# Grouped-query attention with a KV cache on one core: larger transfers, and outputs gathered by four units into token rows

## The chip, the core and the metric

The kernel runs on 1 core of one Trainium2 chip. A core has TensorE (PE; its weight loads are listed as PEld), VectorE (DVE), ScalarE (ACT), GpSimd (POOL) and SyncE (SP, which only issues transfers here), and 16 DMA engines that all transfers share. The metric is the device time of one execution in microseconds (us); less is better.

## The reference

One block of attention over a cache: 8 sequences, 4 new tokens each, model width 512, 32 query heads and 8 heads of K and V (so four query heads share one), 2048 cached positions, head width 128, all bf16. K and V are 32 MiB each, wq and wo 4 MiB each.

```python
B, Sq, D = 8, 4, 512; Hq, Hkv, Sk, Dh = 32, 8, 2048, 128; rep = Hq // Hkv
q = (x @ wq).reshape(B, Sq, Hq, Dh).transpose(0, 2, 1, 3)
k = jnp.repeat(k_cache, rep, axis=1)
v = jnp.repeat(v_cache, rep, axis=1)
scores = jnp.einsum("bhqd,bhkd->bhqk", q, k) * (Dh ** -0.5)
p = softmax(scores, axis=-1)
o = jnp.einsum("bhqk,bhkd->bhqd", p, v)
out = o.transpose(0, 2, 1, 3).reshape(B, Sq, Hq * Dh) @ wo
```

## The kernel before, in words

The work is cut into 8 units: two groups `gg` of four KV heads (G = 4) times four pairs `bp` of sequences (NB = 2). A unit reads 4 MiB of K and 4 MiB of V. The positions of one head are spread over 32 partitions, 64 positions (C) each, so a K or V transfer brings 16 KB to each of 128 partitions.

**Transfers.** All loads are issued by SP, in the order of the list `loads` (L118 to L123): K of unit 0 for its first sequence, x, wq in two halves, the rest of K 0, K 1, and then V of unit u and K of unit u+2 in turn; V of the last unit goes in quarters, wo comes last. Each lands in one of eight slots of 2 MiB of `ring`; `issue` (L125) lets a load go out when its slot's last reader is behind it. The issuing instruction waits on SP until that reader has finished.

**One unit.** `turn` (L162) transposes a piece of K on VectorE, eight pieces of 1.2 us a unit, into six buffers `kt`. `scores` (L185) multiplies them on TensorE with `q_bd`, which holds the queries of a unit in block-diagonal form; `queries` (L172) fills it on GpSimd. `top` (L199) takes the negated maximum on VectorE, `exps` (L221) the exponentials on ScalarE with their sums, `weights` (L235) transposes them on VectorE (`pt`) and copies them into the block-diagonal `p_bd`: of four row groups, three are copied by ScalarE and one by GpSimd. `norm` (L247) inverts the sums. `values` (L255) multiplies with V on TensorE, 64 matmuls a unit, and `scaled` (L272) applies the inverted sums on ScalarE, from PSUM into `o_sb`. `by_heads` (L280) and `to_rows` (L287) bring the result of each unit into `oP` by two matmuls with the permutation `perm`, a copy and a transpose on VectorE; `project` (L298) multiplies with wo.

**Order.** The order is written out by hand: each engine runs its instructions in the order in which the code issues them, and waits on semaphores set by their operands. In iteration u of the main loop (L341) stand the turns and scores of unit u, by_heads of unit u-2, the queries of unit u+1, top, to_rows of unit u-2, exps, weights and norm of unit u, and then values and scaled of unit u-1. So on ScalarE `scaled` of unit u-1 comes after the copies of unit u, and on VectorE the turns of unit u+1 follow norm of unit u. After the loop come the projection of the first head group, the last unit's by_heads and to_rows, the rest of the projection, and the output in two transfers.

Of the kernel before, what the change touches and what calls it, by code (L numbers as in the profile page):

```python
# [12 lines left out]
ALU = mybir.AluOpType  # L13
# [4 lines left out]
def kernel(  # L18
# [31 lines left out]
    DH = D // 2  # L50
    scale = float(Dh) ** -0.5
# [13 lines left out]
    NS = 8  # L65
    pad = ring_pool.tile([128, 192], BF16, name="pad")
    ring = ring_pool.tile([128, NS, C * Dh], BF16, name="ring")
# [3 lines left out]
    perm = const.tile([128, NB, 128], BF16, name="perm")  # L71
# [4 lines left out]
    oP = [const.tile([128, G, 4, NP, NB * Sq], BF16, name=f"oP{i}") for i in range(NG)]  # L76
# [11 lines left out]
    def load_kv(kind, u, b):  # L88
        gg, bp = units[u]
        src = (k_cache if kind == "k" else v_cache)[NB * bp + b, G * gg : G * gg + G]  # L90
        nc.sync.dma_start(  # L91
            ring[:, take((kind, u, b)), :], src.rearrange("g (s c) d -> (g s) (c d)", c=C)
        )

    def load_last_v(u):
        gg, bp = units[u]
        slots = [take(("v", u, b)) for b in range(NB)]
        for h in range(2):
            for b in range(NB):
                src = v_cache[NB * bp + b, G * gg : G * gg + G]  # L100
                nc.sync.dma_start(
                    ring[:, slots[b], h * CH * Dh : (h + 1) * CH * Dh],
                    src.rearrange("g (s c) d -> (g s) (c d)", c=C)[:, h * CH * Dh : (h + 1) * CH * Dh],
                )

    def load_wq(h):
        rows = wq.rearrange("(p r) n -> p (r n)", r=R)
        n = C * Dh
        nc.sync.dma_start(ring[:, take(("wq", h)), :], rows[:, h * n : (h + 1) * n])  # L109

    def load_wo(gg, cuts):
        slot = take(("wo", gg))
        rows = wo[gg * G * 512 : (gg + 1) * G * 512, :].rearrange("(k p r) j -> p k (r j)", k=G, r=4)
        to = ring[:, slot, :].rearrange("p (k n) -> p k n", k=G)
        for g0, g1, r0, r1 in cuts:
            nc.sync.dma_start(to[:, g0:g1, r0 * D : r1 * D], rows[:, g0:g1, r0 * D : r1 * D])

    loads = [("k", 0, 0), ("x",), ("wq", 0), ("wq", 1), ("k", 0, 1), ("k", 1, 0), ("k", 1, 1)]  # L118
    for u in range(NU):
        if u + 2 < NU:  # L120
            loads += [("v", u, 0), ("v", u, 1), ("k", u + 2, 0), ("k", u + 2, 1)]
    loads += [("v", NU - 2, 0), ("v", NU - 2, 1), ("vlast", NU - 1), ("wo", 0), ("wo", 1)]
    loads.reverse()  # L123

    def issue(done):  # L125

        while loads:
            what = loads[-1]
            if what[0] != "x" and n_loads[0] + (what[0] == "vlast") >= done + NS:
                return  # L130
            loads.pop()
            if what[0] in "kv":
                load_kv(*what)
            elif what[0] == "x":
                nc.sync.dma_start(x_sb[:, :], x.flatten_outer_dims())  # L135
            elif what[0] == "wq":
                load_wq(what[1])
            elif what[0] == "vlast":
                load_last_v(what[1])
            elif what[1] == 0:  # L140
                load_wo(0, [(0, 4, 0, 4)])
            else:
                load_wo(1, [(0, 1, 0, 4), (1, 2, 0, 4), (2, 3, 0, 4), (3, 4, 0, 2), (3, 4, 2, 4)])

    issue(0)
# [7 lines left out]
    by_row = ident[:, :].rearrange("k (g b r s) -> k b r g s", g=G, b=NB, r=rep)  # L153
    for b in range(NB):
        nc.gpsimd.tensor_copy(
            out=perm[:, b, :].rearrange("k (r g b s) -> k b r g s", r=rep, g=G, b=NB)[:, b],
            in_=by_row[:, b],
        )
# [3 lines left out]
    def turn(u, b, t):  # L162

        kt = ktpool.tile([128, CT, J, S, 2], BF16, tag="kt", name="kt")
        n = CT * Dh
        nc.vector.transpose(  # L166
            out=kt[:, :, :, :, :].rearrange("w c j s e -> w (c j s e)").bitcast(FP32),
            in_=ring[:, slot_of["k", u, b], t * n : (t + 1) * n].bitcast(FP32),
        )
        kts[u, b, t] = kt  # L170
# [28 lines left out]
    def top(u, h):  # L199
        if h == 0:  # L200
            stats[u] = [small.tile([128, n], FP32, tag=f"stat{i}", name=f"stat{i}") for i, n in enumerate((2, 1, 2, 1))]
        nc.vector.tensor_reduce(  # L202
            out=stats[u][0][:, h : h + 1],
            in_=s_ps[:, 2 * h : 2 * h + 2, :].rearrange("q t n -> q (t n)"),
            axis=AX,
            op=ALU.max,
            negate=True,
        )
        if h == 1:
            nc.vector.tensor_scalar(  # L210
                out=stats[u][1][:, :],
                in0=stats[u][0][:, 0:1],
                scalar1=stats[u][0][:, 1:2],
                scalar2=scale,
                op0=ALU.min,
                op1=ALU.mult,
            )
# [17 lines left out]
    def weights(u, h):  # L235
        pt = small.tile([128, CH // 2, 32, 2], BF16, tag="pt", name="pt")
        nc.vector.transpose(  # L237
            out=pt[:, :, :, :].rearrange("s c q e -> s (c q e)").bitcast(FP32),
            in_=ps[u, h][:, :, :, :].rearrange("q c s e -> q (c s e)").bitcast(FP32),
        )  # L240
        pb = pbs[u, h] = p_bd[(2 * u + h) % 4]
        for g in range(G):
            rows = slice(g * 32, (g + 1) * 32)
            copy = nc.gpsimd.tensor_copy if g == G - 1 else nc.scalar.copy
            copy(out=pb[rows, :, g, :, :], in_=pt[rows, :, :, :])  # L245

    def norm(u):  # L247
        nc.vector.tensor_tensor(
            out=stats[u][3][:, :], in0=stats[u][2][:, 0:1], in1=stats[u][2][:, 1:2], op=ALU.add
        )  # L250
        nc.vector.reciprocal(stats[u][3][:, :], stats[u][3][:, :])
# [3 lines left out]
    def values(u, h):  # L255
        if h == 0:
            o_pss[u] = psum_o.tile([128, NB, Dh], FP32, tag="o", name="o_ps")
        a, b = (slot_of["v", u, i] for i in range(NB))
        v = (ring[:, a : b + 1 : b - a, :] if b > a else ring[:, a : (b - 1 if b else None) : b - a, :])
        v = v.rearrange("p b (c d) -> p b c d", d=Dh)  # L260
        for i in range(CH):
            nc.tensor.matmul(  # L262
                o_pss[u][:, :, :],
                lhsT=pbs[u, h][:, i // 2, :, :, i % 2].rearrange("s g q -> s (g q)"),
                rhs=v[:, :, h * CH + i, :],
                start=(h == 0 and i == 0),
                stop=(h == 1 and i == CH - 1),
            )
# [3 lines left out]
    def scaled(u):  # L272
        o_sb = o_sbs[u] = small.tile([128, NB, Dh], BF16, tag="o_sb", name="o_sb")
        nc.scalar.activation(  # L274
            out=o_sb[:, :, :], in_=o_pss[u][:, :, :], func=COPY, scale=stats[u][3][:, :]
# [4 lines left out]
    def by_heads(u):  # L280
        o_pm = o_pms[u] = psum_m.tile([128, Dh], FP32, tag="m", name="o_pm")
        for b in range(NB):
            nc.tensor.matmul(  # L283
                o_pm[:, :], lhsT=perm[:, b, :], rhs=o_sbs[u][:, b, :], start=(b == 0), stop=(b == NB - 1)
            )

    def to_rows(u):  # L287
        gg, bp = units[u]
        o_r = small.tile([128, 4, 32], BF16, tag="o_r", name="o_r")
        nc.vector.tensor_copy(  # L290
            out=o_r[:, :, :], in_=o_pms[u][:, :].rearrange("q (d r) -> q r d", r=4)
        )
        nc.vector.transpose(
            out=oP[gg][:, :, :, bp, :].rearrange("d g r t -> d r g t"),
            in_=o_r[:, :, :].rearrange("q r d -> q (r d)"),
        )

    def project(gg, g, r0, n):  # L298
        w = ring[:, slot_of["wo", gg], :].rearrange("p (k r j) -> p k r j", k=G, r=4)
        for r in range(r0, r0 + n):  # L300
            for half in range(2):
                nc.tensor.matmul(  # L302
                    out_ps[half * T : (half + 1) * T, :],
                    lhsT=oP[gg][:, g, r, :, :].rearrange("d p t -> d (p t)"),
                    rhs=w[:, g, r, half * DH : (half + 1) * DH],
                    start=(gg == 0 and g == 0 and r == 0),
                    stop=(gg == NG - 1 and g == G - 1 and r == 3),
# [10 lines left out]
    for gg in range(NG):  # L318
        psq = psum_o.tile([128, rep * Dh], FP32, tag="o", name="psq")
        for r in range(R):  # L320
            w = ring[:, slot_of["wq", r // 2], :].rearrange("p (r n) -> p r n", r=2)[:, r % 2, :]
# [19 lines left out]
    for u in range(NU + 1):  # L341
        if u < NU:
# [5 lines left out]
            if u >= 2:  # L348
                by_heads(u - 2)
# [4 lines left out]
            if u >= 2:  # L354
                to_rows(u - 2)
# [5 lines left out]
        if u >= 1:  # L361
            values(u - 1, 0)
            if u == NU:
                by_heads(u - 2)
                to_rows(u - 2)
            values(u - 1, 1)
            scaled(u - 1)
        issue(4 + 4 * u)
    project(0, 0, 0, 4)
    project(0, 1, 0, 4)  # L370
    by_heads(NU - 1)
    to_rows(NU - 1)
    project(0, 2, 0, 4)
    project(0, 3, 0, 4)
    for g in range(G):
        project(1, g, 0, 4)
# [35 lines left out]
```

## Time and profile before

| | |
|---|---|
| time, median of 3 runs | 191.75 us (186.32 to 191.85) |
| time of the profiled execution | 186.44 us |
| span of the profiled execution | 184.3 us |
| mean granted TensorE clock | 0.953 |
| busy: TensorE, VectorE, ScalarE, GpSimd | 136.6, 117.3, 78.2, 36.2 us |
| moved by DMA | 75.71 MB, 411 GB/s over the span |
| transfers issued by SP | 16 of K, 18 of V, 2 of wq, 6 of wo, 1 of x, 1 of the output |

The span runs from the first to the last instruction; the execution's time also holds what lies around it. A slice line of the page cuts the span into 40 equal slices of 4.6 us and gives the busy share in tenths. A line of the timeline gives start, duration, engine, source line, operation, output and inputs, and in brackets how long the engine stood idle before it and which instruction ended that.

### The profile page before, as it was taken

To read this page: it belongs to the slowest core of one execution; us is meant where nothing else is said; L and a number is where in the kernel's file an instruction comes from. 1 tells how busy PE (TensorE), PEld (TensorE's weight loads), DVE (VectorE), ACT (ScalarE), POOL (GpSimd) and SP (SyncE) were. 2 spreads that over 40 slices of the span, in tenths; PEclk is the share of its full clock that TensorE was granted. 3 is DMA by queue.
4 is the path that set the end of the run, shared out by engine and by line. 5 is a ranking of instruction groups with operands and counts; after the bars stand their busy time and mean duration, and the time that the engine had idled before them with its cause. 6 is when DMAs were issued, how large, how long until landed. Compare 5 with 4: busy or idle time off the path is not lost.

```text
span 184.3 us, 2298 instructions
## 1 busy us (share of the span) xinstructions
PE 136.6 (74%) x884; PEld 81.5 (44%) x884; DVE 117.3 (64%) x147; ACT 78.2 (42%) x93; POOL 36.2 (20%) x92
## 2 busy tenths in 40 slices
PE   0001799039997998989759994989498949997992
PEld 0000233013683376338523771368135823486880
DVE  6680290689649976977488666976497549661110
ACT  2000200494079219905950298019900891059410
POOL 8500420080025005200800061005200210003000
PEclk9999999957999999999987999999979996999999
DMA  5999999999999999999999999999999999999980
GB/s 192 430 430 434 437 423 437 427 430 430 427 437 430 425 434 420 439 430 430 427 427 434 427 443 427 423 430 427 444 427 430 430 420 441 414 430 409 421 344 11
DMA packets 6586, 75.71 MB, mean 411 GB/s; under 512 B 720, under 2 KB 816, under 8 KB 1968
## 3 DMA queue, kind: packets, MB, share of 16 engines
q1 hardware_dynamic: 6528, 75.55, 96.6%
q8 instruction: 7, 0.11, 0.2%
q10 hardware_dynamic: 48, 0.02, 0.0%
q14 instruction: 3, 0.02, 0.0%
HBM read 75.53 MB, written 0.03 MB: 410 GB/s over the span
## 4 chain that ended last, share of the span: by engine, by line
DMA 68%; DVE 12%; PE 9%; issue 4%; ACT 3%; POOL 1%; SPq 1%; ACTq 0%; DVEq 0%; POOLq 0%
DMA ring<-in_k_cache_dram 43%; DMA ring<-in_v_cache_dram 17%; PE s_ps L189 9%; DVE kt L166 8%; DMA ring<-in_wo_dram 8%; DVE stat L202 3%; ACT p_sb L223 2%; POOL p_bd L245 1%; DVE pt L237 1%; SPq L109 1%; DVE stat L210 0%; SPq L135 0%; PE out_ps L302 0%; SPq L91 0%; ACT out_sb L379 0%
## 5 line engine op out<-in xcount | busy, mean ns | idle before, releaser
L189 PE MATMUL s_ps<-kt,q_bd 128*128 128x512 bf16 x256 | 70.5, 420 | 23.9 <-DVE kt L166 10.3
L166 DVE STREAM_TRANSPOSE kt<-ring 128x1024 f32<-128x1024 f32 x64 | 73.5, 1210 | 11.9 <-DMA ring<-in_k_cache_dram 11.9
L262 PE MATMUL o_ps<-ring,p_bd 128*128 128x256 bf16 x512 | 57.3, 272 | 3.2 <-DMA ring<-in_v_cache_dram 2.0
L189 PEld LDWEIGHTS <-q_bd 128*128 128x128 bf16 x256 | 25.9, 103 | 67.5 <-issue 31.6
L262 PEld LDWEIGHTS <-p_bd 128*128 128x128 bf16 x512 | 49.8, 98 | 9.9 <-issue 4.1
L223 ACT ACTIVATE p_sb<-s_ps,stat 128x1024 bf16<-128x1024 f32 x16 | 22.0, 1402 | 75.5 <-DVE stat L210 75.5
L245 ACT COPY p_bd<-pt 32x1024 bf16<-32x1024 bf16 x48 | 49.9, 1040 | 0.5
L245 POOL COPY p_bd<-pt 32x1024 bf16<-32x1024 bf16 x16 | 16.6, 1038 | 115.7 <-DVE pt L237 113.2
L202 DVE TENSOR_REDUCE stat<-s_ps 128x1 f32<-128x1024 f32 x16 | 18.9, 1220 | 13.3 <-PE s_ps L189 13.3
L237 DVE STREAM_TRANSPOSE pt<-p_sb 128x512 f32<-128x512 f32 x16 | 11.4, 711 | 15.0 <-ACT p_sb L223 15.0
L178 POOL COPY q_bd<-qT 32x64 bf16<-32x64 bf16 x64 | 13.0, 229 | 15.4 <-DVE qT L334 13.6
L323 PE MATMUL psq<-ring,xT_sb 128*32 128x512 bf16 x32 | 3.8, 626 | 8.2 <-DMA ring<-in_wq_dram 8.2
L290 DVE CAST o_r<-o_pm 128x128 bf16<-128x128 f32 x8 | 2.3, 284 | 10.1 <-PE o_pm L283 10.1
L314 PE MATMUL xtp<-ident,x_sb 32*128 32x32 bf16 x4 | 0.3, 192 | 8.9 <-DMA x_sb<-in_x_dram 8.9
L149 DVE MEMSET p_bd<- 128x2048 uint32 x3 | 5.3, 1765 | 2.0 <-PEq L396 1.2
L334 DVE STREAM_TRANSPOSE qT<-q_sb 128x64 f32<-128x64 f32 x8 | 1.2, 212 | 7.9 <-ACT q_sb L330 7.9
L330 ACT CAST q_sb<-psq 128x512 bf16<-128x512 f32 x2 | 1.2, 585 | 11.2 <-PE psq L323 11.2
L323 PEld LDWEIGHTS <-xT_sb 128*32 128x32 bf16 x32 | 1.2, 129 | 10.0 <-issue 9.5
L274 ACT ACTIVATE o_sb<-o_ps,stat 128x256 bf16<-128x256 f32 x8 | 3.8, 474 | 4.1 <-issue 3.9
L302 PE MATMUL out_ps<-ring,oP 128*32 128x256 bf16 x64 | 4.1, 273 | 0.2 <-DMA ring<-in_wo_dram 0.2
L314 PEld LDWEIGHTS <-x_sb 32*128 32x128 bf16 x4 | 0.2, 114 | 8.9 <-DMA x_sb<-in_x_dram 8.9
L302 PEld LDWEIGHTS <-oP 128*32 128x32 bf16 x64 | 3.0, 96 | 1.1 <-issue 0.6
(20 smaller groups left out, 21.9 us busy)
## 6 DMA issues: line engine op xcount, KB each, us to landing
ring<-in_k_cache_dram SPq DMA_DIRECT2D x16, 2048.0 KB, 27.1
ring<-in_v_cache_dram SPq DMA_DIRECT2D x14, 2048.0 KB, 30.1
ring<-in_wq_dram SPq DMA_DIRECT2D x2, 2048.0 KB, 14.1
ring<-in_v_cache_dram SPq DMA_DIRECT2D x4, 1024.0 KB, 29.4
ring<-in_wo_dram SPq DMA_DIRECT2D x1, 2048.0 KB, 26.9
ring<-in_wo_dram SPq DMA_DIRECT2D x3, 512.0 KB, 22.1
ring<-in_wo_dram SPq DMA_DIRECT2D x2, 256.0 KB, 15.7
x_sb<-in_x_dram SPq DMA_DIRECT2D x1, 32.0 KB, 7.7
```

What stands on the lines that cost most here:

```text
L149: nc.vector.memset(t[:, :, :, :, :], 0.0)
L166: nc.vector.transpose(out=kt[:, :, :, :, :].rearrange("w c j s e -> w (c j s e)").bitcast(FP32), in_=ring[:, slot_of["k", u, b], t * n : ( ...
L178: nc.gpsimd.tensor_copy(out=qb[rows, b, :, g, b, :].rearrange("w (j e) q -> w j e q", e=2), in_=qT[rows, gg, :, NB * bp + b, :, :, :].rear ...
L189: nc.tensor.matmul(s_ps[:, t, :], lhsT=q_bd[u % 2][:, b, 2 * j + e, :, :, :].rearrange("w g b q -> w (g b q)"), rhs=kts[u, b, t][:, :, j, ...
L202: nc.vector.tensor_reduce(out=stats[u][0][:, h : h + 1], in_=s_ps[:, 2 * h : 2 * h + 2, :].rearrange("q t n -> q (t n)"), axis=AX, op=ALU.max,
L223: nc.scalar.activation(out=p_sb[:, :, :, :].rearrange("q c s e -> q c e s"), in_=s_ps[:, 2 * h : 2 * h + 2, :].rearrange("q t (c e s) -> q ...
L237: nc.vector.transpose(out=pt[:, :, :, :].rearrange("s c q e -> s (c q e)").bitcast(FP32), in_=ps[u, h][:, :, :, :].rearrange("q c s e -> q ...
L245: copy(out=pb[rows, :, g, :, :], in_=pt[rows, :, :, :])
L262: nc.tensor.matmul(o_pss[u][:, :, :], lhsT=pbs[u, h][:, i // 2, :, :, i % 2].rearrange("s g q -> s (g q)"), rhs=v[:, :, h * CH + i, :], st ...
L274: nc.scalar.activation(out=o_sb[:, :, :], in_=o_pss[u][:, :, :], func=COPY, scale=stats[u][3][:, :])
L302: nc.tensor.matmul(out_ps[half * T : (half + 1) * T, :], lhsT=oP[gg][:, g, r, :, :].rearrange("d p t -> d (p t)"), rhs=w[:, g, r, half * D ...
L323: nc.tensor.matmul(psq[g * T : (g + 1) * T, :], lhsT=xT_sb[:, r, :], rhs=w[:, (gg * G + g) * rep * Dh : (gg * G + g + 1) * rep * Dh], star ...
```

## The change

- A load of K or V brings both sequences of the unit, 4 MiB in one transfer, into one of four slots of 4 MiB; wq comes in one transfer of 32 KB a partition.
- The first K is issued as two halves of its first sequence, then x in four transfers of 12, 10, 6 and 4 rows, then wq, then its second sequence. The last V is issued in two halves of the positions, both sequences in each.
- wo lies with 16 rows a partition (16 KB); its first half comes in one transfer, its second in four.
- `norm` multiplies the inverted sums with `of_b`, a mask of which rows belong to which sequence. `scaled` scales the first sequence's half on ScalarE, and VectorE then scales the second half and adds the first: one instruction that reads ScalarE's output.
- `by_heads` becomes `by_tokens`: four matmuls, one for each query head of a group, that accumulate four units in one PSUM tile. `to_rows` runs once for four units, over 512 columns, and `oP` holds 16 row groups for all 32 tokens.
- In the last unit one of the copies into `p_bd` goes from ScalarE to VectorE.

The order of the calls in the main loop stays as it was, but for to_rows.

```diff
-    NS = 8
+    NS = 4
-    ring = ring_pool.tile([128, NS, C * Dh], BF16, name="ring")
+    ring = ring_pool.tile([128, NS, NB, C * Dh], BF16, name="ring")
...
+    def load_kv(kind, u, parts):
         gg, bp = units[u]
+        slot = take((kind, u))
+        src = (k_cache if kind == "k" else v_cache)[NB * bp : NB * bp + NB, G * gg : G * gg + G]
+        rows = src.rearrange("b g (s c) d -> (g s) b (c d)", c=C)
+        n = C * Dh
+        for b0, b1, h0, h1 in parts:
+            h0, h1 = int(h0 * n), int(h1 * n)
+            yield nc.sync.dma_start(ring[:, slot, b0:b1, h0:h1], rows[:, b0:b1, h0:h1])
+
+    def load_x():
+        rows = x.flatten_outer_dims()
+        t = 0
+        for n in (12, 10, 6, 4):
+            nc.sync.dma_start(x_sb[t : t + n, :], rows[t : t + n, :])
+            t += n
+
+    def load_wo():
+        slot = take("wo")
+        for gg, cuts in ((0, (0, RW)), (1, (0, 8, 12, 14, 16))):
+            rows = wo[gg * G * 512 : (gg + 1) * G * 512, :].rearrange("(p r) j -> p (r j)", r=RW)
+            for r0, r1 in zip(cuts, cuts[1:]):
+                nc.sync.dma_start(ring[:, slot, gg, r0 * D : r1 * D], rows[:, r0 * D : r1 * D])
+
+    loads = ["k0", "wq", ("k", 1)]
     for u in range(NU):
+        loads.append(("v", u))
+        if u + 2 < NU:
+            loads.append(("k", u + 2))
+    loads.append("wo")
...
     for b in range(NB):
+        nc.vector.tensor_reduce(
+            out=of_b[:, b : b + 1],
+            in_=ident[:, :].rearrange("k (g b q) -> k b g q", g=G, b=NB)[:, b],
+            axis=mybir.AxisListType.XY,
+            op=ALU.add,
         )
...
             copy = nc.gpsimd.tensor_copy if g == G - 1 else nc.scalar.copy
+            if u == NU - 1 and g == 1:
+                copy = nc.vector.tensor_copy
             copy(out=pb[rows, :, g, :, :], in_=pt[rows, :, :, :])
...
+        nc.vector.reciprocal(stats[u][4][:, :], stats[u][4][:, :])
+        nc.vector.tensor_scalar_mul(stats[u][3][:, :], of_b[:, :], stats[u][4][:, :])
...
     def scaled(u):
         o_sb = o_sbs[u] = small.tile([128, NB, Dh], BF16, tag="o_sb", name="o_sb")
         nc.scalar.activation(
-            out=o_sb[:, :, :], in_=o_pss[u][:, :, :], func=COPY, scale=stats[u][3][:, :]
+            out=o_sb[:, 0, :], in_=o_pss[u][:, 0, :], func=COPY, scale=stats[u][3][:, 0:1]
+        )
+        nc.vector.scalar_tensor_tensor(
+            out=o_sb[:, 1, :],
+            in0=o_pss[u][:, 1, :],
+            scalar=stats[u][3][:, 1:2],
+            in1=o_sb[:, 0, :],
+            op0=ALU.mult,
+            op1=ALU.add,
         )
...
-    def by_heads(u):
+    def by_tokens(u):
+        gg, bp = units[u]
+        if bp == 0:
+            o_pms[gg] = psum_m.tile([128, rep, Dh], FP32, tag="m", name="o_pm")
+        w = 32 - NB * Sq - bp * NB * Sq
+        for r in range(rep):
             nc.tensor.matmul(
+                o_pms[gg][:, r, :],
+                lhsT=perm[:, r, w : w + 128],
+                rhs=o_sbs[u][:, 1, :],
+                start=(bp == 0 and r == 0),
+                stop=(bp == NP - 1),
+                skip_group_check=True,
             )
 
+    def to_rows(gg):
+        o_r = q_sb[:, 0, :, :, :, :].rearrange("k r j w e -> k (r j w e)")
         nc.vector.tensor_copy(
+            out=o_r.rearrange("k (r h g) -> k h g r", r=RW, h=rep),
+            in_=o_pms[gg][:, :, :].rearrange("k h (g r) -> k h g r", r=RW),
+        )
+        nc.vector.transpose(out=oP[gg][:, :, :].rearrange("k r t -> k (r t)"), in_=o_r)
...
             if u >= 2:
-                by_heads(u - 2)
+                by_tokens(u - 2)
...
-            if u >= 2:
-                to_rows(u - 2)
+            if u >= 2 and units[u - 2][1] == NP - 1:
+                to_rows(units[u - 2][0])
...
             values(u - 1, 1)
             scaled(u - 1)
-        issue(4 + 4 * u)
+        issue(2 + 2 * u)
```

Lines of the changed kernel that the prediction names: the turns are L182, the ScalarE and VectorE halves of scaled L291 and L294, the copies into p_bd L263.

## The prediction

> **What bounds the kernel now.** I read the slices of the page first, then the timeline of single units, because an average over the span hides who waits for whom.
>
> ```profile
> DVE  6680290689649976977488666976497549661110
> DMA  5999999999999999999999999999999999999980
> GB/s 192 430 430 434 437 423 437 427 430 430 427 437 430 425 434 420 439 430 430 427 427 434 427 443 427 423 430 427 444 427 430 430 420 441 414 430 409 421 344 11
> ```
>
> The DMA engines are full from the second slice to the last but one, at about 430 GB/s; no engine is. So the transfers set the end now: 75.55 MB at 430 GB/s is 175.7 us of the span of 184.3. A unit (8 MiB of K and V) takes 19.4 us of it: in the timeline the turns (L166) that wait for K start at 92.67, 112.07 and 131.53 us.
>
> Next question: how long would a unit take if data were never late? The timeline of units 3 and 4:
>
> ```profile
> 72.30 9.11 DVE L166 STREAM_TRANSPOSE kt<-ring 128x1024 f32<-128x1024 f32 x8
> ...
> 77.55 0.47 ACT L274 ACTIVATE o_sb<-o_ps,stat 128x256 bf16<-128x256 f32 x1
> ...
> 82.53 2.36 DVE L202 TENSOR_REDUCE stat<-s_ps 128x1 f32<-128x1024 f32 x2 [1.12 <-PE s_ps L189]
> 83.01 7.15 PE L262 MATMUL o_ps<-ring,p_bd 128*128 128x256 bf16 x64 [0.41 <-DMA ring<-in_v_cache_dram]
> ...
> 85.25 1.40 ACT L223 ACTIVATE p_sb<-s_ps,stat 128x1024 bf16<-128x1024 f32 x1 [7.23 <-DVE stat L210]
> ...
> 87.94 6.30 ACT L245 COPY p_bd<-pt 32x1024 bf16<-32x1024 bf16 x6
> ...
> 89.01 1.23 DVE L166 STREAM_TRANSPOSE kt<-ring 128x1024 f32<-128x1024 f32 x1
> ...
> 92.67 8.01 DVE L166 STREAM_TRANSPOSE kt<-ring 128x1024 f32<-128x1024 f32 x7 [2.43 <-DMA ring<-in_k_cache_dram]
> ...
> 94.27 0.47 ACT L274 ACTIVATE o_sb<-o_ps,stat 128x256 bf16<-128x256 f32 x1
> ```
>
> (Columns: start, duration, engine, line, operation, count, idle time before it and what ended it.) The reader should see three things. VectorE is free for the next unit's turns at 89.01, as soon as its softmax work is done. ScalarE is not: its six copies into p_bd run to 94.24, and only behind them comes `scaled` (L274) at 94.27, though its matmuls (L262) ended at 90.16. And nobody is held by that late L274: its reader, by_heads on TensorE, stands behind the next scores. This overlap (turns on VectorE while ScalarE copies) is why compute alone needs only 16.7 us a unit (turns start at 55.57 and 72.30, with the data there already) and can wait for DMA.
>
> **The change, part by part.**
>
> *Larger transfers, wq in one, wo in long rows.* The bytes are the same. The trace's packet records give 611 ns for 16 KB, 309 for 8 KB, 159 for 4 KB and 84 for 2 KB, on each of 16 engines. wo goes from 896 of 4 KB and 256 of 2 KB (10.25 us of the 16 engines) to 128 of 16 KB, 128 of 8 KB, 128 of 4 KB and 256 of 2 KB (9.98): 0.27 us saved. There are 14 transfers fewer, each with a 9 ns completion packet per engine: 0.13. K in halves costs 0.06. So -0.3 us, if transfers set the end. Waiting for 4 MiB in place of 2 delays one turn of eight, since the second turn already needed the other sequence.
>
> *Head.* x takes four issues for one, 0.41 us each on SP (all the SP queue behind moves 1.2 us, plus 0.4 for the second half of K), hidden while the first K's 2 MiB still lands (to 8.67 us; without that cover 1.6 us). Eight copies into perm and a wider memset on POOL: under 2 us (copies of 237 ns now), in the 13.6 us that POOL idles before L178. Two small reductions (of_b) on VectorE stand before the first turn; that turn's product is not needed until 23.3. But wq in one transfer moves eight matmuls (1.04 us at 13.63) behind its landing at 18.47: q, POOL's query copies and the first scores come about 0.9 us later. With the new multiplication in norm (about 0.2, as L210) unit 1's first turn goes from 38.44 to 39.5 (bounds 38.6 and 40.1).
>
> *scaled in two, half of it on VectorE.* This decides. ScalarE scales sequence 0 (128x128), then VectorE multiplies sequence 1 and adds ScalarE's result. In the built program both stand at the end of the iteration: on ScalarE behind the six copies, as before; on VectorE behind norm(u) and **ahead of the eight turns of unit u+1**, and the instruction waits for ScalarE. Queued behind it on VectorE are these turns; scores on TensorE wait for the turns, the maximum for the scores, exp for the maximum, the copies for exp, and the next scaled for the copies. The overlap closes into a loop, priced from rows, from first turn S to first turn of the next unit:
>
> - S to the start of the maximum (L202): 72.30 to 82.53 = 10.23 with TensorE busy just before; 38.44 to 49.08 = 10.64 after 7.8 us of idle TensorE, where the granted clock was 0.50 from 37.3 to 44.1. In the new loop TensorE idles about 6 us (values end 7.7 after the maximum's start, scores begin 13.6 after it), so 10.64.
> - Start of the maximum to the end of the copies, where scaled starts: 82.53 to 94.27 = 11.74; it is 11.73 or 11.74 in units 1 to 6.
> - ScalarE's 128x128: no row. Bounds 0.265 (L317, a 128x128 copy) and 0.474 (L274, twice the elements). I take 0.37.
> - Semaphore to VectorE: 0.05 (0.03 to 0.12 between such pairs).
> - VectorE's 128x128 with two inputs: no row. Bounds 0.2 (0.28 of L290, less 0.08 by which a turn overlaps the instruction ahead) and 0.6 (twice L290, for two inputs). I take 0.25.
>
> Sum 23.05 us a unit (22.45 to 23.57) against 19.4 that the transfers need. The transfers stop being the bound; their slots (K free at the last turn, V at the last matmul) come free in time. There are six such loops, from unit 1's first turn to unit 7's: 39.5 + 6 x 23.05 = 177.8. The last maximum starts at 188.4.
>
> TensorE's half clock is the one term that a general rule bears on. The Trainium skill ("TensorE: Matmul & The Clock Gate", Part 1: The HAM clock gate) says that about 3.4 us of idleness halve the clock and about 3.4 us of work restore it; by it all six loops start cold, as I have it, and warm ones would give 212.0. The trace puts the point lower: idle gaps of 2.56 (before 93.97) and 2.74 us were followed by 0.5, one of 2.30 was not, and a half-clock stretch was 3.41 or 6.83 us.
>
> *Gathering by four units.* by_tokens issues four matmuls a unit for two (0.27 us for two): +0.25 on TensorE, in its idle time. CAST and transpose (L290, L293: 0.6 us) leave six of eight units, in VectorE time that is now wait. At the end they are four times as wide: CAST 0.68 (between L290's 0.284 and the 1.22 of 128x1024 in L202, by elements), transpose 0.71 (as L237; bounds 0.31 and 1.24).
>
> *Tail from the last maximum M.* Copies begin at M+5.4 (82.53 to 87.94), now four on ScalarE (1.05 each): M+9.6; in this unit one copy of each half goes to VectorE behind its transpose, and by POOL's 1.04 for the same copy it is done before ScalarE's second. values(6) end at M+7.7; values of unit 7's first half (3.65) at M+11.4; by_tokens(6) 0.5; second half at M+15.6. scaled 0.1+0.37+0.05+0.30, beside 16 matmuls of project (1.05, to M+16.6); by_tokens(7) to M+17.1; CAST and transpose to M+18.6; 32 matmuls of project (44 in 2.69 now) to M+20.55. From the end of TensorE to the end of the span it is 180.92 to 184.33 = 3.41. Span 188.4 + 23.95 = 212.4.
>
> The profiled execution took 186.44 for its span of 184.3, so 2.1 lie around it: **214.5 us**. The median shown, 191.75, is 5.3 above that execution (the runs are 186.32 to 191.85); if whatever adds that also adds here, it is 219.8.
>
> **The rivals.**
>
> *Transfers stay the bound (not slower).* VectorE is busy 64% of the span, so 7 us a unit are free, and the wait could vanish in them. It would if the loop were at most 19.4 us. Then the time is 186.44 - 0.3 = 186.1. Against it: the free time is not where the wait is; the loop is a chain of dependencies, and even its low bound is 22.45. It would need the two unknown terms and 3 us more to be nothing. Chance 0.04, half of it counted as faster because of the distance to the median.
>
> *VectorE waits for the matmuls alone.* If ScalarE's half ran when values end (M+7.7), ahead of the copies, the loop would be 10.64+7.7+0.7 = 19.0, and the time about 186 to 190. The built order has it behind the copies. 0.01.
>
> *Fewer transfers save time each.* If transfers had a gap between them, 14 fewer could give over 2%; it would take 0.27 us each. The landings are 4.83 to 4.90 us apart, and 128 packets of 611 ns on 16 engines are 4.89: no gap. By itself: the Trainium skill ("DMA: Bandwidth & Descriptors", Anatomy of one DMA) has a fixed 2.0 us a transfer, which would be 28 us here if it were not overlapped. 0.01.
>
> *A longer loop.* If the half clock lasted through all 32 score matmuls (428 ns each), S to the maximum would be 1.2+13.7 = 14.9, and 6 x 4.3 more give 240. The longest half-clock stretch was 6.83 us, part of it idle. 0.04.
>
> **How the numbers follow.** Forecast 0.90: 214.5. With all loop terms low, the early head and a tail 1 us shorter: 214.5-3.6-0.9-1 = 209; all high: 214.5+3.1+0.6+1 = 219.2, and 219.8 by the median's distance. Range 208.5 to 220.5. Two per cent is about what a measurement of this kernel can tell from no change. Slower 0.94, same 0.03, faster 0.03.
>
> **What the changed profile would show.** Turns (L182) that start 23 us apart, each behind the new VectorE instruction (L294), which waits for ScalarE's L291 about 5.6 us a unit (from the end of norm, 89.01 in the lines above, to 94.6); in the list of waits this pair is long and that for K is gone. GB/s in the middle near 8.39 MB / 23.05 us = 364, DMA slices with 7 to 8. PEclk dips in every unit. A turn that waits for K's landing in the middle of the run, or 430 GB/s throughout, would prove it wrong.

## The result and the profile after

The changed kernel takes 219.22 us (median of 6 runs, 218.72 to 223.16), the kernel before 189.09 (median of 6, 186.30 to 193.49). The medians hold a few disturbed executions, before above all; the ratio of the undisturbed ones is 1.176 (95% interval 1.173 to 1.178). The profiled execution took 219.11 us for a span of 217.2; the forecast was 214.5 and 212.4.

From the page of the changed kernel: VectorE, TensorE's granted clock, the DMA engines and GB/s by slice (here 5.43 us each), and the chain that ended last.

```profile
DVE  6921825986369534965196537969296529846060
PEclk9999998599958997699959985799559995899987
DMA  6999999999999999999999999789995999400000
GB/s 234 448 465 395 432 435 428 435 432 425 432 429 430 428 429 427 435 432 432 432 429 428 407 409 413 320 341 428 326 413 213 425 391 402 153 3 0 3 0 6
PE 42%; ACT 27%; DVE 19%; DMA 7%; issue 2%; SPq 1%; ACTq 0%; DVEq 0%
```

DMA was 68% of the chain and is 7%: the slices fall to nothing after the 35th (190 us), and the last 27 us of the span pass without transfers, save that of the output. VectorE's row shows the loop: a stretch at 8 or 9 (the turns), a lower one of two or three slices, then 9 again. From the list of waits (engine and line, what it waited for; total, times, longest):

```profile
PE s_ps L205 <- DVE kt L182: 40.9, 6, 7.6
DVE o_sb L294 <- ACT o_sb L291: 35.4, 8, 5.3
```

And the timeline of one loop, the counterpart of the unit shown before:

```profile
84.05 0.37 ACT L291 ACTIVATE o_sb<-o_ps,stat 128x128 bf16<-128x128 f32 x1
84.45 0.35 DVE L294 SCALAR_TENSOR_TENSOR o_sb<-o_ps,stat,o_sb 128x128 bf16<-128x128 f32 x1 [5.32 <-ACT o_sb L291]
84.72 9.12 DVE L182 STREAM_TRANSPOSE kt<-ring 128x1024 f32<-128x1024 f32 x8
...
86.10 9.61 PE L205 MATMUL s_ps<-kt,q_bd 128*128 128x512 bf16 x32 [6.62 <-DVE kt L182]
...
95.75 2.36 DVE L218 TENSOR_REDUCE stat<-s_ps 128x1 f32<-128x1024 f32 x2 [1.90 <-PE s_ps L205]
95.77 7.15 PE L279 MATMUL o_ps<-ring,p_bd 128*128 128x256 bf16 x64
...
101.15 6.31 ACT L263 COPY p_bd<-pt 32x1024 bf16<-32x1024 bf16 x6
...
102.22 1.04 POOL L263 COPY p_bd<-pt 32x1024 bf16<-32x1024 bf16 x1 [0.30 <-DVE stat L266]
102.36 0.92 DVE L270 TENSOR_SCALAR stat<-of_b,stat 128x2 f32<-128x2 f32 x1
...
107.49 0.37 ACT L291 ACTIVATE o_sb<-o_ps,stat 128x128 bf16<-128x128 f32 x1
107.89 0.35 DVE L294 SCALAR_TENSOR_TENSOR o_sb<-o_ps,stat,o_sb 128x128 bf16<-128x128 f32 x1 [4.61 <-ACT o_sb L291]
```

VectorE's softmax work ends at 103.28, but the next turns start only at 108.16, behind L294, which waits for L291, which stands behind ScalarE's copies. The value matmuls it reads had ended at 102.92. Meanwhile TensorE has nothing either: it stands idle 6.62 us before this unit's scores, and 40.9 us before those of six units. First turns stand at 39.07, 61.72, 84.72, 108.16, 131.81, 156.51 and 179.90 us, 22.65 to 24.70 apart.

The end of the span shows a second thing that was not in the kernel before:

```profile
206.00 1.05 PE L332 MATMUL out_ps<-ring,oP 128*32 128x256 bf16 x16
...
207.42 2.39 DVE L322 CAST q_sb<-o_pm 128x512 bf16<-128x512 f32 x1 [0.51 <-PE o_pm L311]
209.84 0.71 DVE L326 STREAM_TRANSPOSE oP<-q_sb 128x512 bf16<-128x512 bf16 x1
...
210.61 3.59 PE L332 MATMUL out_ps<-ring,oP 128*32 128x256 bf16 x32 [2.25 <-DVE oP L326]
```

The gathering CAST takes 2.39 us, and the 32 matmuls behind it run at a little over half their pace: 16 take 1.05 before the wait, 32 take 3.59 after it, at a granted clock of 0.52.

### The profile page after: what moved, and what is told of

It is laid out like the page before. It is cut to its first block, busy times and chain, and to the rows that moved or that the text cites. A ratio compares the mean times of both kernels' runs of the same rounds, so it can differ in the third digit from the quotient of the medians.

```text
span 217.2 us, 2327 instructions
## 1 busy us (share of the span) xinstructions
PE 142.7 (66%) x900; PEld 85.2 (39%) x900; DVE 129.5 (60%) x155; ACT 75.5 (35%) x91; POOL 37.6 (17%) x98
## 4 chain that ended last, share of the span: by engine, by line
PE 42%; ACT 27%; DVE 19%; DMA 7%; issue 2%; SPq 1%; ACTq 0%; DVEq 0%
PE s_ps L205 31%; ACT p_bd L263 17%; ACT p_sb L239 9%; DVE stat L218 8%; DVE kt L182 7%; DMA ring<-in_wq_dram 7%; PE o_ps L279 7%; PE out_ps L332 2%; PE psq L353 2%; DVE q_sb L322 1%; ACT o_sb L291 1%; DVE o_sb L294 1%; DVE stat L226 1%; SPq L106 1%; DVE pt L253 1%
## 5 line engine op out<-in xcount | busy, mean ns | idle before, releaser
L205 PE MATMUL s_ps<-kt,q_bd 128*128 128x512 bf16 x256 | 75.3, 462 | 50.9 <-DVE kt L182 40.9
L182 DVE STREAM_TRANSPOSE kt<-ring 128x1024 f32<-128x1024 f32 x64 | 73.2, 1209 | 0.1
L205 PEld LDWEIGHTS <-q_bd 128*128 128x128 bf16 x256 | 28.0, 112 | 97.4 <-issue 67.3
L263 ACT COPY p_bd<-pt 32x1024 bf16<-32x1024 bf16 x46 | 47.9, 1040 | 1.3 <-DVE pt L253 0.8
L263 POOL COPY p_bd<-pt 32x1024 bf16<-32x1024 bf16 x16 | 16.9, 1062 | 145.7 <-DVE pt L253 143.4
L294 DVE SCALAR_TENSOR_TENSOR o_sb<-o_ps,stat,o_sb 128x128 bf16<-128x128 f32 x8 | 2.8, 351 | 35.4 <-ACT o_sb L291 35.4
L194 POOL COPY q_bd<-qT 32x64 bf16<-32x64 bf16 x64 | 13.0, 229 | 14.9 <-DVE qT L364 13.1
L332 PE MATMUL out_ps<-ring,oP 128*32 128x256 bf16 x64 | 5.7, 346 | 2.2 <-DVE oP L326 2.2
L270 DVE TENSOR_SCALAR stat<-of_b,stat 128x2 f32<-128x2 f32 x8 | 5.7, 714 | 0.3
L332 PEld LDWEIGHTS <-oP 128*32 128x32 bf16 x64 | 3.8, 121 | 3.7 <-DVE oP L326 2.5
L322 DVE CAST q_sb<-o_pm 128x512 bf16<-128x512 f32 x2 | 4.8, 2408 | 0.5 <-PE o_pm L311 0.5
```

Of the source, the lines that this page charges most:

```text
L182: nc.vector.transpose(out=kt[:, :, :, :, :].rearrange("w c j s e -> w (c j s e)").bitcast(FP32), in_=ring[:, slot_of["k", u], b, t * n : ( ...
L194: nc.gpsimd.tensor_copy(out=qb[rows, b, :, g, b, :].rearrange("w (j e) q -> w j e q", e=2), in_=qT[rows, gg, :, NB * bp + b, :, :, :].rear ...
L205: nc.tensor.matmul(s_ps[:, t, :], lhsT=q_bd[u % 2][:, b, 2 * j + e, :, :, :].rearrange("w g b q -> w (g b q)"), rhs=kts[u, b, t][:, :, j, ...
L270: nc.vector.tensor_scalar_mul(stats[u][3][:, :], of_b[:, :], stats[u][4][:, :])
L322: nc.vector.tensor_copy(out=o_r.rearrange("k (r h g) -> k h g r", r=RW, h=rep), in_=o_pms[gg][:, :, :].rearrange("k h (g r) -> k h g r", r ...
L332: nc.tensor.matmul(out_ps[half * T : (half + 1) * T, :], lhsT=oP[gg][:, r, :], rhs=w[:, r, half * DH : (half + 1) * DH], start=(gg == 0 an ...
```

## Experiments

Theory W, the prediction's: VectorE's wait ahead of the turns makes the loop. Rivals: T, the larger transfers; G, the gathering; V, any wait of VectorE for TensorE's values ahead of the turns.

**Move one instruction (e1).** The changed kernel, with L294 behind the turns:

```diff
     def scaled(u):
         nc.scalar.activation(out=o_sb[:, 0, :], ...)
+    def add(u):
...
         nc.vector.scalar_tensor_tensor(out=o_sb[:, 1, :], ..., in1=o_sb[:, 0, :], ...)
...
             if u >= 2:
+                add(u - 2)
                 by_tokens(u - 2)
```

> The changed kernel with one instruction moved: VectorE's half of scaled (the multiply-add that reads ScalarE's half) of unit u-2 is issued behind the eight turns of unit u, just ahead of by_tokens(u-2), instead of ahead of the turns. Theory W (the wait on VectorE closes a loop of 22.65 to 24.7 us a unit): the loop opens, units run at the 19.4 us of the transfers again, GB/s back to 430 through the middle; the end is then set by the changed tail, 26.1 us from the last maximum (at about 160.5): span 186.6, time about 188.6 (187 to 190.5). Rival T (the 4 MiB transfers, their slots and the wait for both sequences cost the time): nothing changes, 217 to 220. Rival G (the gathering, with its wide copies and twice the matmuls): 215 to 220.

Measured: 188.63 us (median of 5), ratio to before 1.013 (1.011 to 1.016); the profiled execution 186.83. Thirty microseconds hang on the place of eight instructions of 0.35 us. Timeline of e1:

```profile
91.95 9.13 DVE L182 STREAM_TRANSPOSE kt<-ring 128x1024 f32<-128x1024 f32 x8 [1.57 <-DMA ring<-in_k_cache_dram]
...
94.58 0.37 ACT L291 ACTIVATE o_sb<-o_ps,stat 128x128 bf16<-128x128 f32 x1
101.00 0.32 DVE L297 SCALAR_TENSOR_TENSOR o_sb<-o_ps,stat,o_sb 128x128 bf16<-128x128 f32 x1
...
111.37 1.25 DVE L182 STREAM_TRANSPOSE kt<-ring 128x1024 f32<-128x1024 f32 x1 [1.63 <-DMA ring<-in_k_cache_dram]
```

The turns wait for K's landing again, 19.42 us apart, and the multiply-add (L297 here) follows them without a wait, since L291 has long been done. T and G fall as causes of the loop: all of both is still in this kernel. The 1.3% by which it is still slower than the kernel before go with the order of the CAST, as e5 and e8 show.

**Take ScalarE out of the wait (e2).** Both halves on VectorE, still ahead of the turns:

```diff
-        nc.scalar.activation(
-            out=o_sb[:, 0, :], in_=o_pss[u][:, 0, :], func=COPY, scale=stats[u][3][:, 0:1]
-        )
+        nc.vector.tensor_scalar_mul(o_sb[:, 0, :], o_pss[u][:, 0, :], stats[u][3][:, 0:1])
```

> The changed kernel with both halves of scaled on VectorE, at the same place ahead of the turns: VectorE then waits for the end of the value matmuls (about 7.2 us after the maximum's start) and no longer for ScalarE, which comes free only 11.74 us after it. Theory W with the copies on ScalarE as the price: first turn 7.9 us after the maximum's start instead of 12.4, loop 10.24 + 7.9 = 18.1, below 19.4, so the transfers bound again and the tail decides: 187 to 191. Rival V (any wait of VectorE for TensorE's values ahead of the turns serializes the two, copies or not): 205 to 219. Rivals T and G: 215 to 220.

Measured: 188.30 us (one run). GB/s by slice from the page of e2, and its timeline:

```profile
GB/s 204 471 450 387 436 422 436 443 418 432 439 422 429 437 425 429 430 429 432 429 432 429 436 429 436 425 432 430 432 429 432 429 425 429 422 425 441 402 118 7
...
86.05 2.35 DVE L218 TENSOR_REDUCE stat<-s_ps 128x1 f32<-128x1024 f32 x2 [1.21 <-PE s_ps L205]
86.07 7.15 PE L279 MATMUL o_ps<-ring,p_bd 128*128 128x256 bf16 x64
...
93.47 0.34 DVE L291 TENSOR_SCALAR o_sb<-o_ps,stat 128x128 bf16<-128x128 f32 x1
93.85 0.35 DVE L292 SCALAR_TENSOR_TENSOR o_sb<-o_ps,stat,o_sb 128x128 bf16<-128x128 f32 x1
94.11 9.12 DVE L182 STREAM_TRANSPOSE kt<-ring 128x1024 f32<-128x1024 f32 x8
...
104.36 2.36 DVE L218 TENSOR_REDUCE stat<-s_ps 128x1 f32<-128x1024 f32 x2 [1.12 <-PE s_ps L205]
```

The next turns start 8.06 us after the maximum instead of 12.4, and the next maximum follows at 104.36: a loop of 18.31, below the transfers' 19.4, and bytes move at about 430 GB/s nearly to the end. V's forecast of 205 to 219 fails. A long wait for the matmuls was not put to the test, though: they end at 93.22, before VectorE, busy with its own softmax work, starts L291 at 93.47. By the sum, 1 us more would still fit at this place; what does not fit is the 6.3 us of ScalarE's copies ahead of L291. VectorE does more work here than in the changed kernel (131.7 us busy against 129.5) and the kernel is 31 us faster.

**Add only the wait (e3).** The kernel before, plus one copy on VectorE of what ScalarE's scaled wrote, which by_heads then reads for the first sequence:

```diff
         nc.scalar.activation(out=o_sb[:, :, :], in_=o_pss[u][:, :, :], func=COPY, scale=...)
+        o_cs[u] = small.tile([128, Dh], BF16, tag="o_c", name="o_c")
+        nc.vector.tensor_copy(out=o_cs[u][:, :], in_=o_sb[:, 0, :])
...
```

> The kernel before with one instruction more and nothing else: after ScalarE's scaled, VectorE copies 128x128 of its output, and by_heads reads this copy for the first sequence. The copy stands ahead of the next unit's turns, as the new instruction does in the changed kernel. Theory W: six loops of 10.9 + 11.74 + 0.65 = 23.3 from 38.4, last maximum at 189, and the tail of before (17.9 to the last transpose, then 48 matmuls and 3.4): span 213 to 215, time 213 to 217, most of what the whole change cost. Rivals T and G: within 2 us of before, 186 to 188.

Measured: 214.49 us (one run). Timeline of e3:

```profile
84.50 0.47 ACT L275 ACTIVATE o_sb<-o_ps,stat 128x256 bf16<-128x256 f32 x1
85.01 0.20 DVE L279 COPY o_c<-o_sb 128x128 bf16<-128x128 bf16 x1 [5.67 <-ACT o_sb L275]
85.12 9.12 DVE L166 STREAM_TRANSPOSE kt<-ring 128x1024 f32<-128x1024 f32 x8
...
108.69 0.20 DVE L279 COPY o_c<-o_sb 128x128 bf16<-128x128 bf16 x1 [5.67 <-ACT o_sb L275]
```

Eight copies of 0.2 us add 28 us to the kernel before. Without one byte of transfers changed, the loop is there: turns at 85.12 and 108.80, six loops of 23.23 on average, the last maximum at 188.98.

**Change only the transfers (e4).** The kernel before with the loads of K, V, x and wq as changed (wo in its old layout and pieces):

```diff
...
+        rows = src.rearrange("b g (s c) d -> (g s) b (c d)", c=C)
+        nc.sync.dma_start(ring[:, slot, b0:b1, h0:h1], rows[:, b0:b1, h0:h1])
...
-        issue(4 + 4 * u)
+        issue(2 + 2 * u)
```

> The kernel before with the changed transfers of K, V, x and wq (4 MiB each, four slots, K 0 in halves, x in four) and nothing else; wo keeps its layout and pieces, in one slot of 4 MiB, and the computation is that of before. Theory W: the transfers cost and bring nearly nothing: 14 completions fewer (0.1 us), first units about 0.6 us later, in cover: 185.8 to 186.8. Rival T: 210 to 220.

Measured: 185.63 us (median of 9), ratio 0.997 (0.996 to 0.998): a gain of 0.3%, and 0.2 us below the range that theory W gave. T is wrong in sign.

What is left of the loop's length and of the tail was split by four more kernels. S and H are the theories on the two terms that the prediction had too small.

**The other order of the CAST, in e1 (e5, e8) and in the changed kernel (e6).**

```diff
-            out=o_r.rearrange("k (r h g) -> k h g r", r=RW, h=rep),
-            in_=o_pms[gg][:, :, :].rearrange("k h (g r) -> k h g r", r=RW),
+            out=o_r.rearrange("k (r h g) -> k r h g", r=RW, h=rep),
+            in_=o_pms[gg][:, :, :].rearrange("k h (g r) -> k r h g", r=RW),
```

> The kernel of e1 (VectorE's half of scaled behind the turns) with the CAST of to_rows written in the other order: it walks through its 512 outputs in the order in which they lie and reads PSUM with a stride, instead of reading in order and writing bf16 with a stride of 64 bytes. Theory S (the strided write makes the 2.4 us): the CAST takes about 0.7, the tail of e1 gets 1.7 us shorter, and the last piece of wo sets the end as in before: 185.2 to 186.5, no slower than before and about level with e4. Rival R (512 columns of PSUM take 2.4 us in either order): as e1, 187 to 189.

> The changed kernel with the CAST in the other order and nothing else, the wait of VectorE left in place. Theory S: 1.7 us less in the tail, 0.9 less in unit 5 (where the CAST stands ahead of the transposes of the weights), and up to 1.6 less because TensorE idles only 0.5 us ahead of its last 32 matmuls, which then run at full clock (1.95 instead of 3.59): 214.5 to 217. Rival R: 218.5 to 219.5.

Measured: e5 185.54 us (median of 5; for a ratio see e8), e6 214.78 (one run). The tail of e6:

```profile
206.49 0.69 DVE L322 CAST q_sb<-o_pm 128x512 bf16<-128x512 f32 x1 [0.51 <-PE o_pm L311]
...
207.98 1.92 PE L332 MATMUL out_ps<-ring,oP 128*32 128x256 bf16 x32 [0.55 <-DVE oP L326]
```

Same values, same shapes: 2.39 us become 0.69. S holds, R falls. TensorE's idle gap is cut from 2.25 to 0.55 us, and its matmuls keep their pace; that the shorter gap is the reason is not shown, since in e1 they kept it after a gap of 2.24 us:

```profile
179.98 1.92 PE L335 MATMUL out_ps<-ring,oP 128*32 128x256 bf16 x32 [2.24 <-DVE oP L329]
```

By the three steps named in the expectation, 1.70 + 1.67 + 0.94 = 4.3 us are saved, and 4.3 is the difference of the times; but that sum is partly luck: unit 1's first turn happened to come 1.27 us earlier in e6, and its seven stretches from first turn to maximum were 1.25 us longer in all (77.90 against 76.65).

> The kernel of e5 once more, with more rounds, for a ratio to the kernel before. Theory: all of the change but the wait and the strided CAST is worth what e4 was worth or a little more: ratio 0.993 to 0.998, 185.0 to 185.9. Rival: the gathering adds work that shows, ratio 1.00 or above.

Measured: 185.67 us (median of 12), ratio 0.995 (0.993 to 0.998). This version is faster than both kernels, if only by half a percent than the one before: the whole change, with one instruction behind the turns and the CAST in the order of its output. Against e4 (0.997) the gain of the gathering and of wo's layout is not resolved.

**Keep TensorE busy (e7), and both (e9).**

```diff
             scaled(u - 1)
+            if u < NU - 1:
+                for _ in range(26):
+                    nc.tensor.matmul(s_ps[:, NT - 1, :], lhsT=ident[:, :], rhs=qT[:, 0, ...], start=True, stop=True)
```

> The changed kernel with 26 matmuls of 128x512 more per unit, which stand behind the value matmuls and fill TensorE's idle time up to the next scores; their results are overwritten by the scores and not used. Theory H (the loop is longer than the predicted 10.64 from first turn to maximum because TensorE runs its first scores at half clock after each idle stretch): the way from first turn to maximum falls from 10.24 to 11.36 to 10.24 in every unit, 5.0 us less in all: about 214.1 (213.5 to 216). Rival D (the scores are paced by the turns on VectorE, and the rest of the loop is elsewhere): 218.5 to 220; and if the added matmuls run into the scores, longer still.

Measured: 214.00 us (one run). Two loops' way from first turn to maximum, in the changed kernel and then in e7 (window, its length, busy time of TensorE, its weight loads, VectorE, ScalarE and GpSimd, then granted clock, DMA share, GB/s):

```profile
84.72:95.75 11.03, 9.65 (x36) 3.85 (x37) 9.13 (x10) 0.00 (x0) 0.00 (x0) 0.71 1.01 432
108.16:119.40 11.24, 9.86 (x36) 3.89 (x37) 9.12 (x9) 0.00 (x0) 0.00 (x0) 0.70 1.00 426
```

```profile
84.28:94.53 10.25, 8.65 (x38) 3.34 (x37) 9.13 (x10) 0.00 (x0) 0.00 (x0) 1.00 1.01 435
106.94:117.18 10.24, 8.64 (x38) 3.34 (x37) 9.12 (x9) 0.00 (x0) 0.00 (x0) 1.00 1.01 434
```

With 26 matmuls more in each of six units the kernel is 5.1 us faster. VectorE is busy 9.12 us in both; the clock is 1.00 instead of 0.7, and the way is 10.24 or 10.25 in all six units that have the added matmuls. H holds: these six ways shrink by 5.0 us in all (66.41 to 61.45). That the times differ by about as much is partly luck, since two differences ahead of the added matmuls cancel. Unit 1, which has no added matmuls ahead of it, took 11.36 in this run and 10.24 in the changed kernel, 1.1 more, and its first turn came at 37.86 instead of 39.07, 1.2 earlier.

> The changed kernel with the additions of e6 and e7 together (CAST in the other order; matmuls that keep TensorE busy), the wait of VectorE left in place. If the terms add up, what is left is the loop of the wait alone: 10.24 + 11.74 + 0.67 = 22.65 us a unit, 219.1 - 4.3 - 5.1 = 209.7 (209 to 211). If one of them hid the other, 212 to 214.

Measured: 210.48 us (one run). Two first turns of e9:

```profile
107.66 9.12 DVE L182 STREAM_TRANSPOSE kt<-ring 128x1024 f32<-128x1024 f32 x8
...
130.31 1.23 DVE L182 STREAM_TRANSPOSE kt<-ring 128x1024 f32<-128x1024 f32 x1
```

All first turns stand at 39.68, 62.33, 85.00, 107.66, 130.31, 152.97 and 175.63: loops of 22.65 to 22.67, within 0.02 of 10.24 + 11.74 + 0.67 = 22.65. From unit 1's first turn to the end of the span it is 168.9 us (208.6 - 39.7) against 178.1 in the changed kernel: 9.2 less, with 5.0 from the clock in the loops and 4.2 from the CAST and what hangs on it.

## Why the prediction was right in its mechanism and wrong in its size

The direction, the mechanism and its place were right: L294 ahead of the turns, L291 behind the copies, transfers no longer the bound. The size was wrong: 28.1 us over the profiled execution of before were forecast (214.5 - 186.44) and 32.7 measured (219.11 - 186.44), a ratio of 1.175 where 1.151 was expected. Two steps failed.

- **The sum.** The span came out 4.8 us too short, because two prices were too low: TensorE's half clock (2.2 us in seven stretches from first turn to maximum, 1.6 in the last matmuls) and the CAST of the gathering (1.7 in the tail, 0.9 in unit 5). The head (0.4) and the rest of the tail (1.2), forecast too long, took back 1.6.
- **The base.** The forecast of 0.90 is the median shown over the predicted time, 191.75 / 214.5. But 214.5 was built on the profiled execution of before, and in proportion to that one it is 186.44 / 214.5 = 0.87. Measured is 186.44 / 219.11 = 0.85, less than even the upper bound leaves of the median (191.75 / 220.5 = 0.87).

The time itself, 219.22 us, is just what the sum gave with all its terms high (219.2), but that is luck: the two prices without a row came as taken, and what was long is listed above.

The 4.8 us of the span, term by term:

| term | forecast | measured | off by |
|---|---|---|---|
| unit 1's first turn | 39.5 | 39.07 | -0.4 |
| six times first turn to maximum | 63.8 | 65.4 | +1.6 |
| six times maximum to scaled | 70.4 | 71.4 | +0.9 |
| six times scaled to next first turn | 4.0 | 4.0 | 0 |
| unit 7, first turn to maximum | 10.64 | 11.21 | +0.6 |
| last maximum to end of span | 23.95 | 26.09 | +2.1 |

- **Half clock.** The step took 10.64 from one row after 7.8 us of idleness, as if this were a fixed price. The seven stretches of the changed kernel are 10.24 to 11.36, those of e6 up to 11.45, and 10.24 with TensorE kept busy: a start at half clock costs between 0 and 1.2 us. The row was one draw of these. The rival of a half clock through all 32 score matmuls (14.9 us) did not come. The Trainium skill ("TensorE: Matmul & The Clock Gate", Part 1) has the activity window run freely, without a restart when a kernel starts, so that it matters where in the window the first matmul falls; a price that varies agrees with that, though no run here moved the phase on purpose. The half clock also reached the last 32 matmuls, 3.59 against the forecast's 1.95: the sum priced them at full clock behind a wait for VectorE.
- **The CAST.** The forecast scaled 0.68 by elements from rows that write in order. The new one writes bf16 64 bytes apart, and takes 2.39 (2.43 in unit 5). In unit 5 that pushed the transposes of the weights back, and made the one interval of 12.68 where 11.74 was taken: "in VectorE time that is now wait" overlooked that the CAST stands ahead of pt, which is on the loop. The Trainium skill ("SBUF — State Buffer", Door 1: The DMA port swizzle) says that accesses that move to a new 16-byte line each time pay a penalty. e6 agrees for the writes, which move on by 64 bytes each time; its reads from PSUM, 64 bytes apart, cost nothing visible (0.69).
- **Exact:** the 11.74 (in five of six units), and the unknown prices: L291 0.37 as taken, L294 0.35 with the next turn 0.27 behind its start (0.25 taken). L294 waits 4.6 to 5.3 us a unit where 5.6 was forecast.
- **The sign that failed:** GB/s near 364 and DMA slices of 7 to 8 through the middle. The transfers stay above 400 GB/s from the fifth slice to the 25th (136 us). The loops are 23.5 us long on average, so compute falls behind by some 4 us a unit, and the transfers first use up the lead that the ring gives them; only then do they wait. SP's issues show this: from 48.22 us on, the loads of K go out 22.6 to 23.7 us apart (at 48.22, 70.86, 93.87, 117.31 and 140.96), while the bytes of a unit still move in 19.5 us at 430 GB/s. A bound that has moved need not show in the slices of the old one for five units. No run varied the ring.
- **Transfers.** -0.3 us was forecast for all of them, 0.27 of it for wo's rows. e4, which keeps wo as it was and issues 13 transfers fewer, measured 0.7 less; where that comes from stays open. For the rival that fewer transfers save time each, this is 0.05 us a transfer at most, where 0.27 was needed.
- **The median.** The 5.3 us between the median shown and the profiled execution were added to the upper bound. The changed kernel's median lies 0.1 us above its profiled execution: that distance did not carry over, and the proportion to the profiled execution was the one to state.

Of the rivals, "transfers stay the bound" failed at its own condition, a loop of at most 19.4. e2 shows that the condition was the right one: with 18.3 the transfers are the bound again. For a dependence on the matmuls alone the second rival had a loop of 19.0; e2, which brings that about in another way, has 18.3. The prediction's way to see through the busy shares, following one instruction's queue on two engines, is what e1 and e3 confirm: 30 us off by moving it, 28 us on by adding it.

## What to carry to other kernels

Before splitting an operation over two engines, list what stands behind each half on its own in-order queue: a cheap instruction that waits for another engine's long queue holds everything after it, and it can close a chain that two iterations had overlapped. Price such a loop by adding the rows around it once, and place the waiting half behind the next iteration's independent work. Don't scale a copy's price by elements when its output order changes: the strided write took 2.39 us here, the one in order 0.69. And state a change in proportion to the execution that the sum was built on.

## What the hardware did that was not expected

- A 128x512 CAST from PSUM to bf16 took 2.39 to 2.43 us written at a stride of 64 bytes and 0.69 read at a stride and written in order.
- Granted clock: an idle gap of 2.25 us ahead of the last 32 matmuls was followed by half pace in the changed kernel (3.59 us) and by full pace in e1 after 2.24 us (1.92). The gap alone doesn't decide it.
- The 128x2 multiplication in norm (L270) takes 0.23 us in the two units where GpSimd is idle and 0.77 to 0.92 in the six where it copies: in the loop shown it ends at 103.28, GpSimd's copy of 1.04 us at 103.26. The Trainium skill ("SBUF — State Buffer", SBUF: two separate sides) describes the port pair that the two engines share as an exclusive lock for a whole instruction, against VectorE instructions of a two-port mode or with two inputs in SBUF; this agrees, though which of the two L270 is no run here shows. It cost nothing in the loop, since VectorE waits for ScalarE next; ahead of unit 1's first turn, where no such wait stands, it took 0.85 us for the 0.2 forecast.
